# Linear attention and a gated MLP on one core: steps that wait for transfers issued turns later, weight decoding and VectorE steps pinned, transfers of a head pair merged

## The chip, the cores and the metric

One core of a Trainium2 chip runs the whole program. The metric is the device time of one execution in microseconds; the median of three runs stands for a kernel.

## The reference, cut to what matters

```python
def phi(x):                                   # 8 batches, 8 heads, 576 tokens, head_dim 64
    proj = einsum('bhsd,df->bhsf', x, w_phi)  # 128 features
    proj = proj - max(abs(proj), axis=-1)
    return concatenate([exp(proj), exp(-proj)], axis=-1)
kv  = einsum('bhsf,bhsd->bhfd', phi(k), v)
z   = sum(phi(k), axis=2)
num = einsum('bhsf,bhfd->bhsd', phi(q), kv)
den = einsum('bhsf,bhf->bhs', phi(q), z) + 1e-6
x   = (num / den) as [4608 tokens, 512]
out = ((x @ w_a) * (x @ w_b)) @ w_out         # d_ff = 1536
```

## The kernel before, in words

The program has two parts. In the first, the attention of 32 head pairs (batch b, pair pr) is written as generators whose steps are placed by hand at "turns": `plan(unit, turns)` puts the next step of a unit at a turn, a pair starts 5 turns after the one before (4 from the eighth pair on). In the code's names `pk`, `kd`, `ke` are the k side, `kvps` the sum of features by values, `pq`, `p32`, `qe` the q side and `pn` the numerator with the denominator as its last row. Into the same loop go three other streams: the weights' decoding (they come as 64-bit numbers; each 128x512 slab `raw` needs one ScalarE and at least four VectorE instructions), the first third of the MLP (pass 0) in nine blocks of 512 tokens (`moe_block`: 24 matmuls for each of four slices of `pa` and `pb`, then 48 for `po`, 144 in all), and `ahead`, the decoding of the weights of passes 1 and 2 (tiles `w_1_`, `w32_1_`, `ws_1_`, `keep_1_` and the same with 2), whose results go to DRAM (`kept`). `PACE` says how many steps of MLP work a turn gets, `AHEAD_TURN` and `AHEAD_PACE` the same for `ahead`. In the second part, passes 1 and 2 run with a Winograd scheme in 12 blocks of 768 tokens (`pab`, `po`).

A token's division by its denominator goes through DRAM: `xun` and `den` are stored from `xn`, `reciprocals` loads `den` as 128x9 (`r`), adds and inverts it on VectorE and stores `rec`; `x_chunk` loads `xun` as `x32` and `rec` spread over 64 partitions as `rb`, multiplies, and keeps `x32` in SBUF for the block while a copy goes to `xnorm` for the later passes. A block can start when all pairs of its batches have gone through this.

The turns set only the order in which instructions are traced. A scheduler then orders each engine's queue by its own timing model and may move an instruction ahead of others on its engine. At run time each engine works its queue in order; all transfers are issued from SyncE's queue, also in order. So an instruction that waits for a transfer holds up all that stand behind it.

Of the kernel before, what the change touches and what calls it, by code (L numbers as in the profile page):

```python
# [58 lines left out]
def tile_kernel(ctx, tc, qT, km, kr, vm, vr, w_phi, w_a, w_b, w_out, out):  # L59
# [107 lines left out]
    def k_load(b, pr, a1, a2, ps, consts, st):  # L167
# [5 lines left out]
        nc.sync.dma_start(k32, km[b, pr])  # L173
# [134 lines left out]
    def q_side(b, pr, j, a1, a2, ps, consts, st):  # L308
# [29 lines left out]
        engine("q_sub", b).tensor_tensor(p32, p32, mb, op=ALU.subtract)  # L338
# [10 lines left out]
        xn = a2.tile([P, S], F32, tag="xn", name=f"xn_{u}")  # L349
        for i in range(2):  # L350
# [5 lines left out]
            nc.scalar.copy(xn[: D + 1, tok], pn[: D + 1, :HALF])  # L356
        nc.sync.dma_start(xun[b][h * D : (h + 1) * D], xn[:D])
        nc.sync.dma_start(den[b][h : h + 1], xn[D : D + 1])
        yield

    def reciprocals(b, pr, a1):
# [496 lines left out]
```

## Time and profile before

| | us |
|---|---|
| median of three runs (1341.44 to 1348.44) | 1345.29 |
| the profiled execution: its time / span of its records | 1340.29 / 1338.5 |
| TensorE busy in the span | 1244.7 |
| VectorE busy | 863.4 |
| ScalarE busy | 655.0 |
| mean granted TensorE clock | 0.974 |

TensorE's busy time contains modelled ends, so that it can't be read as work at its peak; a stretch in which it is idle or at a lower clock is still read from it. The attention runs from 0 to about 676 us, pass 0 of the MLP ends at about 766 us, and the two Winograd passes fill the rest.

### The profile page before, as it was taken

Reading aid. Unit: us, or ns where it says so; the run is one execution under the profiler, and the core shown is the slowest. Engines: PE = TensorE matmul, PEld = TensorE weight load, DVE = VectorE, ACT = ScalarE, POOL = GpSimd, SP = SyncE. Lnnn points to the kernel's source line nnn. Section 1 sums busy time; section 2 is a strip of 40 time slices with the busy share of each in tenths; the row PEclk is TensorE's granted clock in tenths of the full one; section 3 lists DMA queues with packets and bytes.
Section 4 is the critical chain, followed back from the end, with each engine's and each line's share of the span. In section 5 each row is a group of like instructions: output and inputs, shape, how many; then the busy total and the mean of one; then the engine's idle time right before and its main releaser. Section 6 shows DMA issues by size and latency. Waiting matters only on the chain.

```text
span 1338.5 us, 18144 instructions
## 1 busy us (share of the span) xinstructions
PE 1244.7 (93%) x6575; PEld 1087.6 (81%) x6575; DVE 863.4 (65%) x1285; ACT 655.0 (49%) x1199; POOL 155.9 (12%) x70
## 2 busy tenths in 40 slices
PE   7899989889889899999949989999999999999997
PEld 5556657668668788788838789999999999999997
DVE  7987779899878766676525154665566555556453
ACT  5765566777776777777613132332233323223320
POOL 3221121122222222222100000000000000000000
PEclk9989999989889899999979999999999999999999
DMA  7656676766765535444263524413428531332221
GB/s 214 193 159 200 195 251 179 215 194 188 230 199 164 152 105 158 117 107 119 79 239 123 187 80 130 125 53 108 140 86 300 182 119 58 119 118 72 71 95 71
DMA packets 144074, 197.25 MB, mean 147 GB/s; under 512 B 60976, under 2 KB 87728, under 8 KB 143984
## 3 DMA queue, kind: packets, MB, share of 16 engines
q1 hardware_dynamic: 143984, 196.09, 47.7%
q8 instruction: 52, 0.85, 0.3%
q14 instruction: 38, 0.31, 0.1%
HBM read 129.68 MB, written 66.36 MB: 146 GB/s over the span
## 4 chain that ended last, share of the span: by engine, by line
PE 62%; DMA 18%; DVE 10%; ACT 4%; issue 4%; SPq 2%; POOL 0%; DVEq 0%; ACTq 0%
PE pab L661 26%; PE po L711 15%; DMA rb<-rec 4%; PE kvps L275 4%; PE po L594 4%; PE pb L579 4%; PE pa L579 3%; PE pn L355 3%; DMA rec<-r 3%; DMA xun<-xn 3%; DMA r<-den 2%; PE pk L223 1%; DMA raw_b<-in_w_b 1%; PE pq L333 1%; DMA raw_a<-in_w_a 1%
## 5 line engine op out<-in xcount | busy, mean ns | idle before, releaser
L337 POOL PARTITION_ALL_REDUCE mb<-p x64 | 155.3, 2427 | 493.4 <-ACT p L334 435.9
L711 PE MATMUL po<-hh,back_o 128*128 128x384 f32 x768 | 172.5, 340 | 6.7 <-ACT hh L153 6.5
L711 PEld LDWEIGHTS po<-hh,back_o 128*128 128x128 f32 x768 | 137.3, 188 | 9.4 <-ACT hh L153 8.1
L579 PE MATMUL pa<-xh,w_a 128*128 128x512 f32 x288 | 108.2, 417 | 25.5 <-ACT xh L153 25.4
L275 PE MATMUL kvps<-ke,vaug 128*65 128x256 f32 x512 | 126.8, 389 | 1.0 <-ACT ke L237 1.0
L579 PE MATMUL pb<-xh,w_b 128*128 128x512 f32 x288 | 104.2, 408 | 0.0
L275 PEld LDWEIGHTS kvps<-ke,vaug 128*65 128x65 f32 x512 | 71.9, 142 | 39.1 <-issue 4.1
L711 PE MATMUL po<-hl,back_o 128*128 128x384 f32 x384 | 99.0, 339 | 0.0
L594 PE MATMUL po<-hh,w_o 128*128 128x512 f32 x288 | 95.0, 401 | 0.6 <-ACT o L597 0.6
L579 PEld LDWEIGHTS pa<-xh,w_a 128*128 128x128 f32 x288 | 55.5, 193 | 39.4 <-ACT xh L153 27.5
L153 ACT CAST hh<-h 128x768 fp32r<-128x768 f32 (+1 forms) x84 | 61.7, 745 | 45.9 <-DVE h L584 32.6
L717 DVE TENSOR_TENSOR o<-po,o 128x768 f32<-128x768 f32 x48 | 45.3, 954 | 56.5 <-DMA o<-part 48.9
L160 DVE TENSOR_TENSOR hl<-h,hh 128x768 fp32r<-128x768 f32 (+1 forms) x84 | 70.5, 846 | 12.5 <-ACT hh L153 12.5
L153 ACT CAST xth<-xs 128x1536 fp32r<-128x1536 f32 x24 | 35.5, 1480 | 86.6 <-PE pab L661 54.8
L160 DVE TENSOR_TENSOR xtl<-xs,xth 128x1536 fp32r<-128x1536 f32 x24 | 42.2, 1758 | 51.6 <-ACT xth L153 51.6
L160 DVE TENSOR_TENSOR qel<-qe,qeh 128x1152 fp32r<-128x1152 f32 x46 | 64.2, 1396 | 15.1 <-ACT qeh L153 14.9
L711 PEld LDWEIGHTS po<-hl,back_o 128*128 128x128 f32 x384 | 69.9, 188 | 0.0
L667 ACT COPY top<-pab 128x768 f32<-128x768 f32 x24 | 19.3, 803 | 100.9 <-PE pab L661 97.6
L341 ACT ACTIVATE qe<-p 128x576 f32<-128x576 f32 x64 | 43.9, 686 | 43.5 <-DVE qel L160 36.8
L594 PEld LDWEIGHTS po<-hh,w_o 128*128 128x128 f32 x288 | 53.7, 188 | 12.6 <-ACT o L597 0.9
L579 PEld LDWEIGHTS pb<-xh,w_b 128*128 128x128 f32 x288 | 54.5, 191 | 11.5
L546 DVE TENSOR_TENSOR x<-x,rb 128x512 f32<-128x512 f32 x36 | 27.4, 761 | 52.9 <-DMA rb<-rec 45.9
(198 smaller groups left out, 3187.9 us busy)
## 6 DMA issues: line engine op xcount, KB each, us to landing
x<-xnorm SPq DMA_DIRECT2D x48, 384.0 KB
o<-part SPq DMA_DIRECT2D x48, 384.0 KB
q<-in_qT SPq DMA_DIRECT2D x92, 144.0 KB
xun<-xn SPq DMA_DIRECT2D x64, 144.0 KB
xnorm<-x SPq DMA_DIRECT2D x36, 256.0 KB
part<-o SPq DMA_DIRECT2D x36, 256.0 KB
part<-o SPq DMA_DIRECT2D x24, 384.0 KB
out_x<-o SPq DMA_DIRECT2D x24, 384.0 KB
```

Source lines behind the costliest of these rows:

```text
L153: eng.copy(dst, src)
L160: eng_lo.tensor_tensor(lo, src, hi, op=ALU.subtract)
L275: nc.tensor.matmul(st["kv_ps", b, pr][:width, j], v_[:, j, :width], e_[:, j], start=(left == NFULL and j == 0 and n_ == 0), stop=(left == ...
L337: nc.gpsimd.partition_all_reduce(mb, p32, P, bass_isa.ReduceOp.absmax)
L341: nc.scalar.activation(e[:, 0], p32, AF.Exp)
L355: nc.tensor.matmul(pn[: D + 1, :HALF], kv_[:, 2 * j + s, :], e_[:, s, tok], **at)
L546: nc.vector.tensor_tensor(x32, x32, rb, op=ALU.mult)
L579: nc.tensor.matmul(acc, w_, x_, start=(k == 0), stop=(k == 3 * NCC - 1))
L594: nc.tensor.matmul(acc, w_, h_, start=(k == 0), stop=(k == 3 * SLICES - 1))
L661: nc.tensor.matmul(acc[to][:, i], w_, x_, skip_group_check=True, **at)
L711: nc.tensor.matmul(acc[cc][:, t], w_, h[:, t], **at)
L717: nc.vector.tensor_tensor(o, acc[cc], o, op=ALU.add)
```

## The change

What it does:

1. `reciprocals` no longer does its work in one turn. Its six steps (load of `r`; add and reciprocal; store of `rec` with the load of `x32`; load of `rb`; multiplication; store of `xnorm`) stand 1, 3, 4, 5, 7 and 8 turns after the pair's last q step (`REC_TURNS`), in the first batch 0, 1, 1, 1, 2 and 2 turns after it.
2. The multiplication is done once for a pair and 576 tokens, and blocks load their `x32` from `xnorm`; the next block's loads are issued in the middle of the one before, if that block is ready by then. A block that was not loaded ahead has two steps more.
3. `behind(loads, ...)` puts these transfers, in SyncE's queue, behind the newest load of q or k, and `behind(marks, ...)` puts the two VectorE steps behind the newest subtraction of `mb` on VectorE.
4. `pinned()` does the same for all that the loop issues as MLP work, decoding and `ahead`: their VectorE instructions come behind the newest such subtraction. What is issued after the attention's loop is not pinned.
5. `ahead` starts at turn 84 instead of 50, with one step a turn instead of 0.6.
6. `xun` and `den` are stored once for a pair instead of once for a head; the host turns the rows of `w_a` and `w_b` to match the new order.
7. q's second copy and the zeros around v's rest come from the host, so that one transfer loads what two did.
8. Blocks start 2 turns behind the last step of a batch instead of 8.

```diff
-DECODE_TURN, X_LAG, BLOCK_LAG = 2, 2, 8
+REC_TURNS0, REC_TURNS, X_TURNS = (0, 1, 1, 1, 2, 2), (1, 3, 4, 5, 7, 8), (2, 3)
+DECODE_TURN, BLOCK_LAG = 2, 2
 PACE0, PACE, PACE0_UNTIL = 0.35, 0.5, 34
-AHEAD_TURN, AHEAD_PACE = 50, 0.6
+AHEAD_TURN, AHEAD_PACE = 84, 1.0
...
-        engine("q_sub", b).tensor_tensor(p32, p32, mb, op=ALU.subtract)
+        marks.append(nc.vector.tensor_tensor(p32, p32, mb, op=ALU.subtract))
...
-            nc.scalar.copy(xn[: D + 1, tok], pn[: D + 1, :HALF])
-        nc.sync.dma_start(xun[b][h * D : (h + 1) * D], xn[:D])
-        nc.sync.dma_start(den[b][h : h + 1], xn[D : D + 1])
-        yield
+            nc.scalar.copy(xn[: D + 1, j, tok], pn[: D + 1, :HALF])
+        if j == 1:
+            nc.sync.dma_start(den[b][h - 1 : h + 1].unsqueeze(0), xn[D : D + 1])
+            nc.sync.dma_start(xun[b][pr * P : (pr + 1) * P].rearrange("(d h) s -> d h s", h=2), xn[:D])
+        yield
...
+    def behind(what, issue):
+
+        with tc.issue_after(what[-1].ins):
+            issue()
...
-        nc.sync.dma_start(r, den[b][hs].rearrange("h (a n) -> (h a) n", n=n))
-        nc.vector.tensor_scalar_add(r, r, EPS)
+        behind(loads, lambda: nc.sync.dma_start(r, den[b][hs].rearrange("h (a n) -> (h a) n", n=n)))
+        yield
+        behind(marks, lambda: nc.vector.tensor_scalar_add(r, r, EPS))
         nc.vector.reciprocal(r, r)
-        nc.sync.dma_start(rec[b][hs].rearrange("h (a n) -> (h a) n", n=n), r)
+        yield
+        behind(loads, lambda: nc.sync.dma_start(rec[b][hs].rearrange("h (a n) -> (h a) n", n=n), r))
+        x32 = a1.tile([P, S], F32, tag="x32", name=f"x32_{b}_{pr}")
+        nc.sync.dma_start(x32, xun[b][pr * P : (pr + 1) * P])
+        yield
+        rb = a1.tile([P, S], F32, tag="rb", name=f"rb_{b}_{pr}")
+        behind(loads, lambda: nc.sync.dma_start(rb, rec[b][hs].unsqueeze(0).broadcast_to([D, 2, S])))
+        yield
+        behind(marks, lambda: nc.vector.tensor_tensor(x32, x32, rb, op=ALU.mult))
+        yield
+        t = 0
+        while t < S:
+            g, t0 = divmod(b * S + t, GROUP)
+            m = min(S - t, GROUP - t0)
+            behind(loads, lambda: nc.sync.dma_start(xnorm[g][pr * P : (pr + 1) * P, t0 : t0 + m], x32[:, t : t + m]))
+            t += m
...
+            plan(reciprocals(b, pr, pools[0]), [t0 + Q_STEP + Q_TURNS[-1] + t for t in (REC_TURNS if b else REC_TURNS0)])
...
+                plan(x_first, [t0 + Q_STEP + Q_TURNS[-1] + t for t in X_TURNS])
...
+                plan(b, [t0 + Q_STEP + Q_TURNS[-1] + REC_TURNS[-1]])
...
-            nc.sync.dma_start(x32[:, dst], xun[b][c * P : (c + 1) * P, src])
...
-                nc.sync.dma_start(rb[i * D : (i + 1) * D, dst], rec[b][h : h + 1, src].broadcast_to([D, n]))
...
-        nc.vector.tensor_tensor(x32, x32, rb, op=ALU.mult)
-        nc.sync.dma_start(columns(xnorm, j * T1, T1)[:, c], x32)
+    def x_load(j, c):
+        x32 = xpool.tile([P, T1], F32, tag="x32", bufs=3, name=f"x32_0_{j}_{c}")
+        nc.sync.dma_start(x32, columns(xnorm, j * T1, T1)[:, c])
         return x32
...
+    def x_make(j, c, x32):
+
+        hl = [xpool.tile([P, T1], F32R, tag=f"x{k}", bufs=NCC, name=f"x{k}_0_{j}_{c}") for k in "hl"]
+        split(*hl, x32, nc.scalar, nc.vector)
+        block_x.setdefault(j, []).append(hl)
...
-            first_x.append(x_)
+            loaded = x_load(0, c)
+            yield
+            x_make(0, c, loaded)
             yield
...
-        xs = first_x if j == 0 else list(load_x(j))
-        hs = []
-        yield
+        if j > 0 and j not in block_x:
+            for c in range(0, NCC, 2):
+                loaded = [x_load(j, c + i) for i in range(2)]
+                yield
+                for i in range(2):
+                    x_make(j, c + i, loaded[i])
+        hs, xs, loaded = [], block_x.pop(j), []
...
+            if f == 1 and j + 1 < blocks[0]:
+                loaded = [x_load(j + 1, c) for c in range(3)]
...
+            if loaded:
+                x_make(j + 1, cc, loaded.pop(0))
+                if cc + 3 < NCC:
+                    loaded.append(x_load(j + 1, cc + 3))
...
+    def pinned():
+
+        return tc.issue_after(marks[-1].ins) if marks else nullcontext()
...
-            run(work, int(due))
-            due -= int(due)
-            if turn >= AHEAD_TURN:
-                due_ahead += AHEAD_PACE
-                while due_ahead >= 1:
-                    next(ahead, None)
-                    due_ahead -= 1
+            with pinned():
+                if work:
+                    run(work, int(due))
+                    due -= int(due)
+                else:
+                    due = 0.0
+                if turn >= AHEAD_TURN:
+                    due_ahead += AHEAD_PACE
+                    while due_ahead >= 1:
+                        next(ahead, None)
+                        due_ahead -= 1
```

TensorE around the numerators of heads 2 and 3 of batch 2 (`pn_2_2`, `pn_2_3`; numbers at names' ends are the program's). Before:

```order
L355 MATMUL pn_2_2_0_1664<-qeh_2_2_1524,kvh_2_1_1576 65x288 x2
L355 MATMUL pn_2_2_1_1672<-qeh_2_2_1524,kvh_2_1_1576 65x288 x2
L333 MATMUL pq_2_5_0_1729<-qs_2_5_1725,wh_118 128x288
L333 MATMUL pq_2_5_0_1729<-qs_2_5_1725,wl_119 128x288
L579 MATMUL pb_0_1_0_2035<-xh_0_1_3_1926,w_0_0_b_249 128x512
L579 MATMUL pa_0_1_1_2135<-xl_0_1_3_1927,w_0_1_a_311 128x512
L579 MATMUL pa_0_1_1_2135<-xh_0_1_3_1926,w_0_1_a_311 128x512
L579 MATMUL pb_0_1_1_2148<-xh_0_1_0_1884,w_0_1_b_400 128x512
L579 MATMUL pb_0_1_1_2148<-xl_0_1_0_1885,w_0_1_b_400 128x512
```

With the change, TensorE's queue at the same numerator:

```order
L331 MATMUL pq_2_5_1_1709<-qs_2_5_1701,wh_118 128x288
L331 MATMUL pq_2_5_1_1709<-qs_2_5_1701,wl_119 128x288
L355 MATMUL pn_2_2_0_1658<-qel_2_2_1508,kvh_2_1_1578 65x288 x2
L355 MATMUL pn_2_2_0_1658<-qeh_2_2_1507,kvl_2_1_1580 65x288 x2
L355 MATMUL pn_2_2_1_1666<-qel_2_2_1508,kvh_2_1_1578 65x288 x2
L355 MATMUL pn_2_2_1_1666<-qeh_2_2_1507,kvl_2_1_1580 65x288 x2
L296 MATMUL pt_2_2_1737<-ident_126,kvT_2_2_1735 128x65 x4
L222 MATMUL pk_2_3_2_1713<-wzh_122,kh_2_3_1542 128x256
L222 MATMUL pk_2_3_2_1713<-wzl_123,kh_2_3_1542 128x256
L222 MATMUL pk_2_3_2_1713<-wzh_122,kl_2_3_1543 128x256
L222 MATMUL pk_2_3_2_1713<-wzh_122,kh_2_3_1542 128x256
```

Before, 52 instructions of MLP block 1 (`pa_0_1`, `pb_0_1`) stand between `pn_2_2` and the first of `pn_2_4`; with the change none does, since block 1's first matmuls come only at head 6 of the batch: block 0 is done by then, and block 1, which was not ready in time to be loaded ahead, has its two loading steps first.

TensorE at the last numerator of the attention, `pn_7_7`, and what stands next (`pa_0_6` is block 6's). Before:

```order
L355 MATMUL pn_7_7_1_6563<-qel_7_7_6533,kvh_7_3_6458 65x288 x2
L355 MATMUL pn_7_7_1_6563<-qeh_7_7_6532,kvl_7_3_6460 65x288 x2
L579 MATMUL pa_0_7_1_6979<-xh_0_7_0_6900,w_0_1_a_311 128x512
L579 MATMUL pa_0_7_1_6979<-xl_0_7_0_6901,w_0_1_a_311 128x512
L579 MATMUL pa_0_7_1_6979<-xh_0_7_0_6900,w_0_1_a_311 128x512
L579 MATMUL pa_0_7_1_6979<-xh_0_7_1_6914,w_0_1_a_311 128x512
L579 MATMUL pa_0_7_1_6979<-xl_0_7_1_6915,w_0_1_a_311 128x512
L579 MATMUL pa_0_7_1_6979<-xh_0_7_1_6914,w_0_1_a_311 128x512
```

With the change, TensorE's queue at the same numerator:

```order
L592 MATMUL pa_0_6_0_6561<-xh_0_6_3_6512,w_0_0_a_197 128x512
L592 MATMUL pa_0_6_0_6561<-xl_0_6_3_6513,w_0_0_a_197 128x512
L355 MATMUL pn_7_7_0_6396<-qel_7_7_6345,kvh_7_3_6251 65x288 x2
L355 MATMUL pn_7_7_0_6396<-qeh_7_7_6344,kvl_7_3_6253 65x288 x2
L355 MATMUL pn_7_7_1_6404<-qel_7_7_6345,kvh_7_3_6251 65x288 x2
L355 MATMUL pn_7_7_1_6404<-qeh_7_7_6344,kvl_7_3_6253 65x288 x2
L592 MATMUL pa_0_6_0_6561<-xh_0_6_3_6512,w_0_0_a_197 128x512
L592 MATMUL pb_0_6_0_6574<-xh_0_6_0_6414,w_0_0_b_270 128x512
L592 MATMUL pb_0_6_0_6574<-xl_0_6_0_6415,w_0_0_b_270 128x512
```

Before, blocks 0 to 6 are done by then and block 7 follows, whose x needs the last pairs of batch 7; with the change the last numerator stands among the first matmuls of block 6, so that 133 of block 6's 144 matmuls come before block 7's first.

VectorE, rows of the decoding for pass 2 (`w_2_`, `w32_2_`, `ws_2_`, `keep_2_`). Before, around the subtraction for head 0 of batch 4 (`p32_4_0`):

```order
L424 SCALAR_TENSOR_TENSOR w_2_1_b_0_8274<-raw_2_2_b_8272,w_2_1_b_0_8274 128x512
L160 TENSOR_TENSOR keep_2_1_w22_2_1_a_8242<-w32_2_1_a_8017,keep_2_1_w22_2_1_a_8242 128x256
L467 TENSOR_TENSOR w32_2_1_b_8271<-w_2_1_b_0_8274 128x512
L338 TENSOR_TENSOR p32_4_0_2879<-p32_4_0_2879,mb_4_0_2978 128x576
L227 TENSOR_REDUCE m_4_1_0_2989<-pk_4_1_0_2981 128x4
L160 TENSOR_TENSOR qel_3_6_2810<-qe_3_6_2806,qeh_3_6_2809 128x1152
L228 TENSOR_TENSOR kd_4_1_0_2988<-pk_4_1_0_2981,m_4_1_0_2989 128x512
L160 TENSOR_TENSOR keep_2_1_b_w1_2_1_b_8442<-w32_2_1_b_8271,keep_2_1_b_w1_2_1_b_8442 128x512
L419 TENSOR_SCALAR w_2_1_b_1_8340<-w_2_1_b_1_8340 128x512
L421 SCALAR_TENSOR_TENSOR w_2_1_b_1_8340<-raw_2_3_b_8338,w_2_1_b_1_8340 128x512
L422 TENSOR_SCALAR w_2_1_b_1_8340<-w_2_1_b_1_8340 128x512
```

With the change, at the same subtraction:

```order
L227 TENSOR_TENSOR kd_4_1_0_2815<-pk_4_1_0_2808,m_4_1_0_2816 128x512
L161 TENSOR_TENSOR qel_3_6_2683<-qe_3_6_2679,qeh_3_6_2682 128x1152
L336 TENSOR_TENSOR p32_4_0_2750<-p32_4_0_2750,mb_4_0_2805 128x576
L383 TENSOR_TENSOR x32_3_1_2785<-x32_3_1_2785,rb_3_1_2821 128x576
L373 TENSOR_SCALAR r_3_2_2823<-r_3_2_2823 128x9
L374 RECIPROCAL r_3_2_2823<-r_3_2_2823 128x9
L166 TENSOR_TENSOR qs_4_2_2936<-q32_4_2_2819,qs_4_2_2936 64x576
L226 TENSOR_REDUCE m_4_1_2_2905<-pk_4_1_2_2897 128x4
```

and behind the attention's last split (`qel_7_7`):

```order
L161 TENSOR_TENSOR qel_7_7_6345<-qe_7_7_6341,qeh_7_7_6344 128x1152
L161 TENSOR_TENSOR keep_2_0_a_w1_2_0_a_6507<-w32_2_0_a_6381,keep_2_0_a_w1_2_0_a_6507 128x512
L441 TENSOR_SCALAR w_2_0_a_1_6444<-w_2_0_a_1_6444 128x512
L383 TENSOR_TENSOR x32_7_2_6394<-x32_7_2_6394,rb_7_2_6438 128x576
L443 SCALAR_TENSOR_TENSOR w_2_0_a_1_6444<-raw_2_1_a_6442,w_2_0_a_1_6444 128x512
L444 TENSOR_SCALAR w_2_0_a_1_6444<-w_2_0_a_1_6444 128x512
L446 SCALAR_TENSOR_TENSOR w_2_0_a_1_6444<-raw_2_1_a_6442,w_2_0_a_1_6444 128x512
L489 TENSOR_TENSOR w32_2_0_a_6381<-w_2_0_a_1_6444 128x512
L494 TENSOR_TENSOR ws_2_0_a_6500<-w32_2_0_a_6381 128x256
```

Counted over the whole queue, up to the subtraction for `p32_2_1`, from there to `p32_4_7`, from there to `p32_7_7`, and behind it: of pass 0's 72 decoding instructions all 72 stay in the first part; of pass 1's 92 there were 55, 37, 0 and 0, and are 0, 10, 79 and 3; of pass 2's 92 all stood in the second part, and all stand behind the attention now. Pass 2's decoding is traced behind the attention in both kernels; its slabs come through the same single buffer `raw` as pass 1's, and behind them.

## Rows read from the trace of the kernel before

**Rows 1.** The page: busy time, share of the span and instructions of each engine.

```profile
PE 1244.7 (93%) x6575; PEld 1087.6 (81%) x6575; DVE 863.4 (65%) x1285; ACT 655.0 (49%) x1199; POOL 155.9 (12%) x70
```

**Rows 2.** Windows by stage: PE, PEld, DVE, ACT, POOL busy, PEclk, DMA share, GB/s.

```profile
0.00:204.00 204.00, 179.45 (x768) 122.55 (x769) 158.19 (x286) 128.03 (x271) 50.44 (x27) 0.97 0.67 201
204.00:452.00 248.00, 225.74 (x1187) 181.39 (x1186) 214.38 (x331) 177.64 (x349) 53.10 (x22) 0.96 0.65 195
452.00:676.00 224.00, 216.69 (x1187) 177.71 (x1186) 146.90 (x210) 157.53 (x311) 52.41 (x21) 0.98 0.42 116
676.00:698.00 22.00, 2.21 (x10) 1.40 (x9) 2.49 (x7) 1.02 (x3) 0.00 (x0) 0.65 0.70 250
698.00:775.00 77.00, 71.98 (x309) 58.94 (x309) 28.23 (x46) 23.07 (x39) 0.00 (x0) 0.97 0.54 174
775.00:1338.00 563.00, 548.63 (x3120) 545.61 (x3120) 313.25 (x410) 167.69 (x230) 0.00 (x0) 0.99 0.35 112
```

**Rows 3.** Waits, 0 to 204 us: who waited for whom, total us, times, longest.

```profile
DVE x L546 <- DMA rb<-rec: 8.6, 5, 2.2
...
DVE r L366 <- DMA r<-den: 4.1, 4, 2.6
```

**Rows 4.** Waits, 204 to 452 us.

```profile
PE pq L333 <- DVE qs L165: 12.6, 4, 5.3
DVE r L366 <- DMA r<-den: 10.3, 8, 3.4
...
DVE x L546 <- DMA rb<-rec: 6.4, 4, 2.2
```

**Rows 5.** Waits, 452 to 676 us.

```profile
DVE r L366 <- DMA r<-den: 31.8, 12, 4.7
...
DVE x L546 <- DMA rb<-rec: 17.2, 6, 4.1
...
PE pq L333 <- DVE qs L165: 4.5, 1, 4.5
```

**Rows 6.** Windows of short stretches inside the attention; columns as in rows 2.

```profile
321.00:345.00 24.00, 22.64 (x121) 18.43 (x120) 23.01 (x39) 18.39 (x37) 4.97 (x2) 1.00 0.67 207
452.00:471.00 19.00, 14.47 (x80) 11.75 (x79) 13.68 (x20) 13.49 (x27) 4.28 (x2) 0.82 0.54 142
471.00:530.00 59.00, 59.00 (x325) 48.70 (x324) 41.87 (x59) 44.25 (x88) 15.51 (x6) 1.00 0.45 129
```

**Rows 7.** VectorE groups, 204 to 452 us: busy us, mean ns, idle before.

```profile
L424 DVE SCALAR_TENSOR_TENSOR w_o<-raw_o,w_o 128x512 f32<-128x512 uint32 x8 | 5.5, 689 | 0.2
...
L160 DVE TENSOR_TENSOR keep_b_sl_b<-ws_b,keep_b_sh_b 128x1024 fp32r<-128x1024 f32 x2 | 3.2, 1578 | 0.0
...
L472 DVE TENSOR_TENSOR ws_b<-w_b 128x256 f32<-128x256 f32 x2 | 0.8, 410 | 0.0
```

**Rows 8.** Timeline of VectorE, 455 to 466 us: start, length, instruction, idle before.

```profile
457.68 0.17 DVE L366 TENSOR_SCALAR r<-r 128x9 f32<-128x9 f32 x1 [3.07 <-DMA r<-den]
```

**Rows 9.** The chain that ended last, 675 to 776 us: start us, us, what.

```profile
682.54 2.82 DMA rec<-r
...
688.77 7.43 DMA rb<-rec
...
751.55 2.80 PE pb L579 x12
```

**Rows 10.** The same chain, 160 to 176 us.

```profile
171.19 3.18 DMA xnorm<-x
```

**Rows 11.** The same chain, a transfer of raw weights.

```profile
255.92 5.12 DMA raw_a<-in_w_a
```

**Rows 12.** Waits of ScalarE for raw weights, whole run.

```profile
ACT w_b L418 <- DMA raw_b<-in_w_b: 19.1, 10, 4.3
...
ACT w_o L418 <- DMA raw_o<-in_w_out: 13.8, 9, 3.4
...
ACT w_a L418 <- DMA raw_a<-in_w_a: 8.3, 7, 2.6
```

More of the change, by code (lines that the diff above doesn't have):

```diff
@@ L2 @@
 from collections import deque
-from contextlib import ExitStack
+from contextlib import ExitStack, nullcontext
 import concourse.bass as bass
@@ L172, in k_load @@
         k32 = a1.tile([P, n], F32, tag="k32", bufs=2, name=f"k32_{u}")
-        nc.sync.dma_start(k32, km[b, pr])
+        loads.append(nc.sync.dma_start(k32, km[b, pr]))
         v32 = vaug[i % 3]
@@ L197, in rest_load @@
         v32 = rvz[g % 2]
-        for r in range(2):
-            rows = slice(r * REST, (r + 1) * REST)
-            nc.sync.dma_start(v32[rows, r, :, :D], vr[b, g, rows])
+        nc.sync.dma_start(v32[:, :, :, :D], vr[b, g])
         yield
@@ L321, in q_side @@
             q32 = a2.tile([P, S], F32, tag="q32", name=f"q32_{u}")
-            for r in range(2):
-                nc.sync.dma_start(q32[r * D : (r + 1) * D], qT[b, h])
+            loads.append(nc.sync.dma_start(q32, qD[b, h]))
             yield
@@ L754, in run @@
                 steps -= 1
-    away, weights, places, first_x, done_ahead = {}, {}, {}, [], set()
+    away, weights, places, block_x, done_ahead, marks, loads, blocks = {}, {}, {}, {}, set(), [], [], [0]
     places_ps, wide_pools, later_pool = [0], [], []
@@ L770, in tile_kernel @@
                 n = (ready + 1) * S // T1
-                tasks[turn + BLOCK_LAG] = [moe_block(j, ps_moe) for j in range(blocks, n)]
-                blocks = n
+                tasks[turn + BLOCK_LAG] = [moe_block(j, ps_moe) for j in range(blocks[0], n)]
+                blocks[0] = n
             for t in sorted(tasks):
@@ L841, with turned @@
     vm = np.ascontiguousarray(vp[:, :, :, :n].reshape(B, H // 2, 2, n // P, P, D).transpose(0, 1, 4, 3, 2, 5))
[L842 removed]
+    vr = np.zeros((B, H // 4, 2, S - n, 2, 2, D), v.dtype)
+    for r in range(2):
+        vr[:, :, r, :, r] = vp[:, r::2, :, n:].transpose(0, 1, 3, 2, 4)
+    vr = vr.reshape(B, H // 4, 2 * (S - n), 2, 2, D)
+    def turned(w):
+        return np.ascontiguousarray(w.reshape(H // 2, 2, D, -1).transpose(0, 2, 1, 3)).reshape(w.shape)
     arrays = {
[L844 to L845 removed]
+        "qP": qP, "qD": qD, "km": km, "kr": kr, "vm": vm, "vr": vr, "w_phi": np.ascontiguousarray(w_phi),
+        "w_a": turned(moe_w_a).view(np.int64), "w_b": turned(moe_w_b).view(np.int64), "w_out": moe_w_out.view(np.int64),
     }
```

42 lines of the change are left out of this document (11 added, 31 removed).

## The prediction

> **What bounds the kernel now.** I read the busy times first [rows 1]: TensorE is busy for 1244.7 of 1338.5 us, no other engine for more than 863. All matmuls are the same with the change, so the time can only fall by what TensorE loses. Then the windows by stage [rows 2]. A stage's loss I reckon as its length less the busy time, plus (1 - granted clock) times its length, since a matmul at half clock takes twice as long:
>
> - 0 to 204: 204 - 179.45 = 24.6, and 0.03 x 204 = 6.1: 30.7 us
> - 204 to 452: 22.3 + 0.04 x 248 = 32.2 us
> - 452 to 676: 7.3 + 0.02 x 224 = 11.8 us
> - 676 to 698: 19.8 us, almost all of it
> - 698 to 775: 5.0 + 2.3 = 7.3 us; 775 to 1338: 14.4 + 5.6 = 20.0 us
>
> That is 122 us. The two Winograd passes are at their limit and the change doesn't touch them, so the question is the first 95 us of the list.
>
> What ends the waits there? Third view: the waits by stage. VectorE waits for `r` and `rb` in all three: 12.7 us [rows 3], 16.7 us [rows 4] and 49.0 us [rows 5]. The reader should see that the stage with most of these waits has the smallest loss: from 452 to 676 VectorE is busy for 146.9 of 224 us [rows 2], so 49 us of waiting fit into its slack, and between 471 and 530 TensorE isn't idle at all [rows 6]. From 204 to 452 it is busy for 214.4 us; with 16.7 of waits that is 231 of 248. In the stretch from 321 to 345 it is busy for 23.0 of 24 [rows 6], and TensorE's longest waits are for `qs`, a VectorE result, 12.6 us [rows 4]. So VectorE's queue is the bound of this stage, and the waits for transfers matter there because they stand in a full queue.
>
> What fills that queue? By the counts in the section on the change 129 decoding instructions, of which 92 are for pass 2. Their durations lie between 410 and 1578 ns, most near 689 [rows 7]; I take 0.65 us each.
>
> **The change part by part.**
>
> *Middle, 204 to 452.* 129 decoding instructions become 10: 119 x 0.65 = 77 us leave VectorE, and most of the 16.7 us of waits, since `r` and `rb` now have about two turns each. Its occupied time falls from 231 to about 138 us, and it no longer bounds. Four head pairs, though, get next to no MLP work (the first place shown is one), and attention alone doesn't fill TensorE: the stretch from 452 to 471, which holds one such pair, loses 4.5 + 0.18 x 19 = 7.9 us [rows 6]. At best such a pair loses nothing, as 471 to 530 does; in the 7.9 there is a 4.5 us wait of TensorE for `qs` [rows 5], and VectorE had stood 3.07 us at `r` some instructions ahead of that `qs` [rows 8], which goes. So I take 2.7 for each, nearer to the low end: 11 us, and 3 us for the seven other pairs. 32 becomes 14: **-18 us** (bounds -29, all losses gone, and +3, four pairs at 7.9 and 3).
>
> *First stage, 0 to 204.* 127 decoding instructions become 72: 55 x 0.65 = 36 us less of VectorE's 158, and 12.7 us of waits. Its start, where nothing else is ready, stays. I take a third of the loss: **-10 us** (bounds 0 and -20).
>
> *Late stage, 452 to 676.* 79 decoding instructions of pass 1 come in: 79 x 0.65 = 51 us. The waits of 49.0 us go. VectorE is occupied for 146.9 + 51 = 198 us instead of 195.9. Nothing changes in sum: **0 us** (bounds: -11.8, and +17 if the stage loses the share that 204 to 452 loses now, 13%).
>
> *Tail, 676 to 698.* The last numerator is now followed by 133 matmuls of block 6. By the pace of 12 in 2.80 us [rows 9] they take 31 us. Behind them stands block 7, which waits for the last pair's chain: store of `den`, `r`, `rec`, `rb`, product, then, new, the store of `xnorm` and its load. The chain took some 22 us (676 to 698) in the kernel before, with `rec` at 2.82 and `rb` at 7.43 us [rows 9]; the store of `xnorm` took 3.18 us [rows 10], the load is taken as the same: 28 us, just under 31. But pass 2's decoding is here now: 92 x 0.65 = 60 us come on top of 28.2 us of VectorE from 698 to 775 [rows 2], in about 100 us of three blocks. That is 88% full, as the middle stage was (86%), so it will cost something: between 0 and 13% of 100 us. I take 8. 19.8 becomes 8: **-12 us** (bounds -20 and -7).
>
> The page "DMA: Bandwidth & Descriptors" of the Trainium skill, section "Anatomy of one DMA", gives a transfer a fixed cost of about 2 us however small it is, which speaks against two more links in the chain; by its figure alone the two would cost 4 us, an estimate, and 26 us would still fit under block 6.
>
> *At nothing.* Merged stores and loads (`xun`, `den`, q, v's rest) take issues from SyncE's queue; SyncE's own time isn't on the path while TensorE is busy, which is the cover, and if that were gone the merged transfer of a pair would start when its second head is done, one q step later than the first head's did. The loads of x for pass 0 (36 of 256 KB) are new traffic; the share of the DMA engines in the stages is 0.67 and below. At the block's start VectorE has a step less, since the product is done before.
>
> **The sum.** -18 - 10 + 0 - 12 = -40 us. The profiled execution took 1340.29 us, 1.8 more than its span, so 1300 us; the median of the runs is 1345.29, 0.4% above it, and 1300.3/1340.29 x 1345.29 = **1305 us**.
>
> **The rivals.**
>
> *The queues run clean (A).* With no wait for a transfer in VectorE's queue every stage runs like 471 to 530. First stage -20, middle -29, late -8, tail -20: -77, 1268 us. For it: the losses are chains of waits, and a stall is followed by a slow clock. Against: the sparse pairs.
>
> *Sparse pairs stall (B).* Attention alone is a chain from engine to engine, and each pair without MLP work loses 7.9 us as from 452 to 471. Four in the middle give +3 there; in the late stage two in place of one, +8; with -10 and -12 that is -11 us: 1334 us. For it: the granted clock of 0.82 in that stretch, while VectorE was busy for only 13.7 of 19 us [rows 6], so that it wasn't VectorE's load that held TensorE. Against: the same stretch held waits that the change removes. "TensorE: Matmul & The Clock Gate" of the Trainium skill, section "What's actually happening", says that an engine which was idle gets half its clock pulses until it has been busy again; by that rule each hole is paid for twice, and the clock of 0.82 behind the idle time there agrees.
>
> *Nothing comes of it (C).* As B, and the decoding in the tail costs block 6 to 8 what the hole of 19.8 cost: -11 + 12 = +1, 1346 us.
>
> *The decoding in the tail binds (D), slower.* There is one `raw` buffer, so a slab's load starts when VectorE is done with the one before, and the decoding stands between the splits that TensorE's `po` matmuls need. A load took 5.12 us [rows 11]. If VectorE stood still for all of it 12 times, that is 61 us: -28 + (61 + 8 - 19.8) = +21, 1367 us. It turns the sign when more than 40 of the 61 us come through, 3.3 us of each load. Against: in the whole run before ScalarE, which is first to touch a slab, waited 41.2 us for 36 slabs [rows 12], 1.1 us each; 12 of these are 14 us, about my 8.
>
> **How the numbers follow.** The forecast has a chance of 0.57, A 0.19, B 0.09, C 0.07, D 0.08. A change of this kernel under 0.5% (6.7 us) can't be told from none. The forecast's own span is 1285 to 1325, its bounds not all at one end; the range, 1268 to 1336, takes in A and B and leaves out C and D. Faster by over 0.5% (under 1338.6): forecast, A and nearly all of B, 0.84. Within 0.5%: C and a rest, 0.08. Slower: D, 0.08.
>
> **What would show it.** In the changed profile: VectorE's waits for `r` and `rb` under 15 us in sum; its busy time per us falls in the second batch to the fourth (under 75%) and rises from the fifth on; the last numerator comes earlier than 676 us by some 60 us (145 MLP matmuls, 34 us at the pace of 12 in 2.80 us, moved behind it, and the 28 us of the first two stages); no idle stretch of TensorE over 5 us behind it. Wrong would be the middle term if the pairs without MLP work show a granted clock under 0.9, and the tail term if `pa` or `po` of blocks 6 to 8 wait for splits by more than 15 us, with VectorE waiting for slabs.

## The result, and the profile after

The changed kernel takes 1293.78 us in the median of four runs (1289.77 to 1296.88), the kernel before 1346.87 beside it: a ratio of 0.961, interval 0.957 to 0.965. 1305 was predicted, in a range of 1268 to 1336. The profiled execution took 1292.23 us; its span is 48 us shorter than the 1338.5 of before.

The page of the changed kernel: the span, then busy time and share of each engine.

```profile
span 1290.4 us, 17768 instructions
PE 1234.2 (96%) x6575; PEld 1086.4 (84%) x6575; DVE 862.1 (67%) x1281; ACT 658.3 (51%) x1199; POOL 152.8 (12%) x70
```

The windows of the changed kernel, cut where the same heads end as in [rows 2]: the first three stages, the tail in two pieces, the Winograd passes.

```profile
0.00:188.00 188.00, 165.81 (x733) 115.57 (x734) 122.04 (x211) 116.20 (x248) 49.26 (x27) 0.97 0.59 171
188.00:381.00 193.00, 186.39 (x1058) 152.89 (x1057) 152.59 (x223) 154.19 (x306) 50.97 (x22) 0.99 0.60 174
381.00:612.00 231.00, 223.12 (x1203) 181.72 (x1202) 194.76 (x300) 172.76 (x338) 52.60 (x21) 0.98 0.67 197
612.00:700.00 88.00, 85.68 (x371) 68.75 (x370) 64.48 (x117) 38.63 (x65) 0.00 (x0) 1.00 0.81 284
700.00:742.00 42.00, 33.69 (x139) 28.61 (x138) 15.75 (x26) 10.88 (x18) 0.00 (x0) 0.84 0.65 220
742.00:1290.00 548.00, 539.48 (x3079) 538.84 (x3077) 312.54 (x408) 165.69 (x226) 0.00 (x0) 0.99 0.36 114
```

By the prediction's formula (length less TensorE's busy time, plus (1 - clock) times length) TensorE's losses are now, with those of before in brackets: first stage 27.8 (30.7), middle 8.5 (32.2), late stage 12.5 (11.8), tail 2.3 + 15.0 = 17.3 (27.1), passes 14.0 (20.0). That is 80 after 122. The clock is read to 0.01, which is 2 us in a stage of 200 and 5.5 us in the passes. The middle gave most of it. VectorE's share there fell from 86% to 79%, and rose from 66% to 84% in the late stage, as the decoding moved.

The losses explain 42 of the 48 us; the lengths close the account. ScalarE has copied the last numerator of the attention at 611.6 us, after 676.1 before. 145 MLP matmuls now come behind it that came ahead of it, 34 us at the pace of [rows 9], an estimate; so the first three stages gained 31 us. From there to the matmul at which TensorE's wait for `top` ends (the passage to the Winograd passes) it is 120.6 us, after 99.3; without the 34 us that is a gain of 12.5. The 3120 matmuls from that one to the end take 558.2 us, after 563.2: a gain of 5.0. Together that is the 48 us. TensorE's waits for `hh` in the passes, the kernel before and then the changed one:

```profile
PE po L711 <- ACT hh L153: 6.5, 5, 2.1
```

```profile
PE po L730 <- ACT hh L154: 2.1, 1, 2.1
```

VectorE's waits for `r` and `rb` in the changed kernel, one stage after the other (total us, times, longest).

```profile
DVE r L373 <- DMA r<-den: 4.9, 4, 3.2
DVE x L383 <- DMA rb<-rec: 4.2, 3, 1.9
...
DVE r L373 <- DMA r<-den: 6.2, 7, 1.7
...
DVE r L373 <- DMA r<-den: 5.1, 3, 2.5
DVE x L383 <- DMA rb<-rec: 1.7, 1, 1.7
```

They are 22 us in the whole run, after 78 in the three stages [rows 3 to 5] (94 with the tail); the late stage holds 6.8 after 49.0. TensorE's own waits in the changed kernel: for block 0's x in the first stage; for `qs` in the middle and the late stage; in the tail.

```profile
PE pa L592 <- ACT xh L154: 7.2, 2, 6.2
...
PE pq L331 <- DVE qs L166: 1.0, 2, 0.5
...
PE pq L331 <- DVE qs L166: 5.3, 3, 2.3
...
PE po L613 <- ACT o L616: 3.9, 1, 3.9
PE pab L680 <- ACT top L686: 3.7, 1, 3.7
```

The 12.6 us for `qs` in the middle [rows 4] have become 1.0. One wait has grown: TensorE's longest wait for block 0's `xh` in the first stage was 2.0 us before and is 6.2 now, as that x goes through the store of `xnorm` and a load.

### The profile page after: what moved, and what is told of

Its sections match the earlier page's. It is cut to its first block, busy times and chain, and to the rows that moved or that the text cites. A ratio compares the mean times of both kernels' runs of the same rounds, so it can differ in the third digit from the quotient of the medians.

```text
span 1290.4 us, 17768 instructions
## 1 busy us (share of the span) xinstructions
PE 1234.2 (96%) x6575; PEld 1086.4 (84%) x6575; DVE 862.1 (67%) x1281; ACT 658.3 (51%) x1199; POOL 152.8 (12%) x70
## 4 chain that ended last, share of the span: by engine, by line
PE 74%; DMA 10%; DVE 8%; issue 3%; ACT 3%; POOL 1%; SPq 0%; POOLq 0%; DVEq 0%; ACTq 0%
PE pab L680 27%; PE po L730 16%; PE kvps L274 8%; PE pn L355 5%; PE pa L592 5%; PE pb L592 5%; PE po L613 4%; PE pk L222 2%; PE pq L331 2%; DMA x<-xnorm 1%; DMA raw_o<-in_w_out 1%; DMA rec<-r 1%; DMA rb<-rec 1%; DMA xnorm<-x 1%; DVE qs L166 1%
## 5 line engine op out<-in xcount | busy, mean ns | idle before, releaser
L335 POOL PARTITION_ALL_REDUCE mb<-p x64 | 152.2, 2379 | 429.0 <-ACT p L332 370.5
L592 PE MATMUL pa<-xh,w_a 128*128 128x512 f32 x288 | 101.4, 407 | 7.2 <-ACT xh L154 7.2
L613 PE MATMUL po<-hh,w_o 128*128 128x512 f32 x288 | 99.0, 410 | 5.1 <-ACT o L616 3.9
L592 PE MATMUL pb<-xh,w_b 128*128 128x512 f32 x288 | 98.4, 398 | 1.5 <-ACT h L596 1.5
L730 PE MATMUL po<-hl,back_o 128*128 128x384 f32 x384 | 99.3, 339 | 0.0
L161 DVE TENSOR_TENSOR qel<-qe,qeh 128x1152 fp32r<-128x1152 f32 x46 | 64.6, 1405 | 16.6 <-ACT qeh L154 16.3
L686 ACT COPY top<-pab 128x768 f32<-128x768 f32 x24 | 19.3, 803 | 105.3 <-PE pab L680 102.9
L166 DVE TENSOR_TENSOR qs<-q,qs 64x576 fp32r<-64x576 f32 x46 | 52.0, 1131 | 28.1 <-ACT qs L154 27.2
L690 ACT COPY top<-pab 128x768 f32<-128x768 f32 x24 | 19.2, 802 | 97.0 <-PE pab L680 97.0
L226 DVE TENSOR_REDUCE m<-pk 128x4 f32<-128x512 f32 x64 | 44.0, 688 | 32.7 <-PE pk L222 32.1
L592 PEld LDWEIGHTS pb<-xh,w_b 128*128 128x128 f32 x288 | 54.1, 188 | 13.9 <-ACT h L596 1.7
```

The lines of the kernel that those rows point to most:

```text
L161: eng_lo.tensor_tensor(lo, src, hi, op=ALU.subtract)
L166: eng_lo.tensor_tensor(hi_lo[D:], src[D:], hi_lo[D:], op=ALU.subtract)
L226: nc.vector.tensor_reduce(out=m[:, : 2 * n], in_=p, op=ALU.max, axis=AX.X, apply_absolute_value=True)
L335: nc.gpsimd.partition_all_reduce(mb, p32, P, bass_isa.ReduceOp.absmax)
L592: nc.tensor.matmul(acc, w_, x_, start=(k == 0), stop=(k == 3 * NCC - 1))
L613: nc.tensor.matmul(acc, w_, h_, start=(k == 0), stop=(k == 3 * SLICES - 1))
```

## The experiments

Two theories. *Queue*: what counts is which instructions stand in VectorE's and ScalarE's queues ahead of those that TensorE waits for; the decoding's way out of the middle is the gain. *Waits*: the gain is that no step waits for a transfer in VectorE's queue, which the spreading does. Ratios are to the kernel before on the same chip; where microseconds are worked out from them, 1340 stands for it. The changed kernel was run once more with the last set. Each edit also lets the scheduler write another order on the other engines, so a run shows the edit with the order that came of it.

| run | median us | ratio [interval] | losses: first, middle, late, tail, passes |
|---|---|---|---|
| before | 1340 to 1347 | 1 | 30.7, 32.2, 11.8, 34.7, 20.0 |
| change | 1293.78 | 0.961 [0.957, 0.965] | 27.8, 8.5, 12.5, 17.1, 14.0 |
| change_again | 1287.77 | 0.961 [0.959, 0.963] | 24.8, 8.6, 11.0, 13.9, 14.3 |
| decode_back | 1321.66 | 0.986 [0.982, 0.990] | 20.2, 30.6, 4.0, 29.7, 20.3 |
| decode_alone | 1300.85 | 0.970 [0.967, 0.973] | 19.3, 18.0, 22.0, 9.0, 14.2 |
| spread_back | 1322.04 | 0.986 [0.981, 0.990] | 32.3, 29.9, 28.9, 9.6, 14.0 |
| unmerged | 1302.61 | 0.972 [0.969, 0.975] | 25.8, 19.4, 10.2, 10.0, 19.7 |
| q_two | 1294.85 | 0.966 [0.963, 0.970] | 31.4, 8.7, 10.6, 14.0, 14.4 |
| x0_direct | 1301.44 | 0.970 [0.967, 0.973] | 26.0, 19.2, 10.8, 11.7, 9.2 |
| held_early | 1299.71 | 0.969 [0.966, 0.973] | 28.8, 18.8, 10.6, 9.7, 8.8 |
| p2_late | 1297.05 | 0.967 [0.965, 0.970] | 28.6, 8.5, 12.5, 8.4, 20.2 |
| p2_slow | 1309.31 | 0.977 [0.975, 0.979] | 30.9, 10.5, 11.0, 10.4, 30.6 |
| qs_behind | 1305.28 | 0.974 [0.971, 0.976] | 29.1, 21.2, 14.2, 16.4, 13.6 |
| blocks_free | 1318.64 | 0.984 [0.981, 0.986] | 16.8, 10.5, 22.7, 43.1, 20.5 |

The losses are by the formula, each kernel cut at its own heads, the tail in one window (so 34.7 for before, where two windows give 27.1). The two profiles of the changed kernel differ by 3 us in the first stage and the tail. p2_late, p2_slow, held_early and qs_behind have its first stage instruction by instruction, and over these six profiles that stage loses 24.8 to 30.9 us: a difference under 6 us there shows nothing. The losses don't add up to the medians, since both terms of the formula count idle time at half clock.

**decode_back.**

```diff
-AHEAD_TURN, AHEAD_PACE = 84, 1.0
+AHEAD_TURN, AHEAD_PACE = 50, 0.6
...
-        return tc.issue_after(marks[-1].ins) if marks else nullcontext()
+        return nullcontext()
```

> The changed kernel with the decoding of the later passes back at turn 50 at a pace of 0.6 and nothing of it held behind a named instruction: 129 decoding instructions stand on VectorE between the last numerators of batches 1 and 4 again, and none in the tail. Spread steps and merged transfers stay. First theory (the gain is VectorE's queue emptied of decoding): about 1322 us, 28 slower than the 1294 of the change; from batch 2 to 4 VectorE is busy for over 85% of the time and TensorE's loss there is 25 us or more again, against 8.5 with the change. Rival (the gain is that no step waits for a transfer in VectorE's queue): about 1302, since the steps stay spread; TensorE's loss in that stage stays under 15 us.

33 us of 52 go (0.9857 - 0.9611 of 1340): *queue* got its number. The middle and the tail, cut from this run's windows:

```profile
187.00:424.00 237.00, 215.91 (x1150) 174.43 (x1148) 205.30 (x321) 174.08 (x343) 52.11 (x23) 0.96 0.69 210
...
649.00:741.00 92.00, 74.62 (x319) 60.22 (x317) 26.90 (x44) 22.45 (x38) 0.00 (x0) 0.91 0.51 168
```

VectorE is at 87% in the middle and TensorE loses 30.6 us, though the steps are still spread and VectorE waits only 6.2 us for `r` there. The hole behind the last numerator is back as well (17.4 us for `xh`), with 16 matmuls of block 6 behind that numerator in place of 133. The edit frees the blocks' steps too; blocks_free, below, frees them alone, and there the hole comes back while the middle loses 10.5. So the hole is theirs, and the middle's loss is the decoding's, with ScalarE's order that came with it (qs_behind). One more thing shows in the order of instructions alone: with the named instructions left out and the numbers 84 and 1.0 kept, each engine's order is line for line that of this kernel. The table of turns does nothing by itself here; the named instruction moves the decoding.

**decode_alone.** The kernel before, with

```diff
-AHEAD_TURN, AHEAD_PACE = 50, 0.6
+AHEAD_TURN, AHEAD_PACE = 84, 1.0
...
-            run(work, int(due))
...
+            with pinned():
+                run(work, int(due))
...
```

> The kernel before, with this alone: the decoding starts at turn 84 at a pace of 1.0, and decoding and blocks' VectorE steps are held behind the last subtraction. The reciprocals, the products in the blocks and the transfers are as before. First theory: about 1318 us, with 10 decoding instructions left in batches 2 to 4, TensorE's loss there 12 us or less, though VectorE still waits for r and rb there. Rival: 1335 to 1346 us, the loss stays 25 or more. As x for block 7 must be made from the last rec inside the block, the hole behind the last numerator should be shorter than 19.8 us by either theory, since matmuls of earlier blocks now stand there.

Three quarters of the gain (0.970), more than *queue* expected. The edit does two things, it moves the decoding and holds the blocks' steps. The middle loses 18.0, not 12, the first stage 19.3. But the late stage, with decoding and waits both in it (VectorE waits 45 us for `r` and `rb` in the whole run, 16 of them there), loses 22.0 in place of 11.8.

**spread_back.**

```diff
-REC_TURNS0, REC_TURNS, X_TURNS = (0, 1, 1, 1, 2, 2), (1, 3, 4, 5, 7, 8), (2, 3)
+REC_TURNS0, REC_TURNS, X_TURNS = (0,) * 6, (0,) * 6, (2, 3)
...
-        with tc.issue_after(what[-1].ins):
-            issue()
+        issue()
...
```

> The changed kernel with the six steps of the reciprocals in one turn and none of them held behind a named instruction; a batch's blocks still start at the same turn. First theory: 1294 to 1302 us; VectorE waits for r and rb come back (40 us or more in sum, most in the late stage), but lie in its slack. Rival: 1320 us or more, with TensorE losing 25 us or more from batch 2 to 4.

*Waits* got its number: 33 us lost, in the middle (29.9) and in the late stage (28.9). Two rows of VectorE's waits in the middle, and the window of that stage:

```profile
DVE x L382 <- DMA rb<-rec: 16.1, 9, 5.9
DVE r L372 <- DMA r<-den: 11.7, 8, 3.4
```

```profile
191.00:405.00 214.00, 196.98 (x1066) 158.97 (x1065) 150.53 (x224) 153.79 (x307) 53.38 (x22) 0.94 0.56 158
```

VectorE is busy for 70% there, 83% with these waits, so that waits can cost as much in a queue that isn't full. One of the two casts named below, that of (4,2), stands behind here as well. The whole run has 73 us of waits for `r` and `rb`. The change puts the product with `rb` into the attention's queue, where the kernel before had it in the blocks. So the spreading isn't a gain over the kernel before, it is what the new place of the product needs: decode_alone, which has neither, is 21 us faster than this one.

**unmerged, q_two.**

```diff
-            loads.append(nc.sync.dma_start(q32, qD[b, h]))
+            for r in range(2):
+                loads.append(nc.sync.dma_start(q32[r * D : (r + 1) * D], qD[b, h, :D]))
...
-        if j == 1:
-            nc.sync.dma_start(den[b][h - 1 : h + 1].unsqueeze(0), xn[D : D + 1])
+        nc.sync.dma_start(den[b][h : h + 1], xn[D : D + 1, j])
```

(the store of `xun` and the rest of v alike; q_two has the first part alone).

> The changed kernel with the transfers of before in place of the merged ones: q in two transfers of 64 rows, the rest of v in two, and each head's numerator and denominator stored when that head is done. Both theories: within 6 us of 1294, since SyncE's queue is not on TensorE's path. A third theory (the merging shortens the chain that TensorE waits for) gives 1305 us or more.

> The changed kernel with q alone loaded in two transfers of 64 rows again. If it was q that cost the 10 us in the middle when all transfers were undone (TensorE's waits for qs, 8 us there): 1300 us or more. If it was the stores of xun and den, or only another order that came with them: 1291 to 1297 us.

Unmerged is 14 us slower than the change, which looked like the third theory. But its middle loses 19.4, and TensorE's longest waits there are again for `qs`, 10.3 us, not for a transfer. The orders of the two kernels differ in where ScalarE's cast to `qs` of heads (2,6) and (4,2) stands: ahead of a cast to `qeh` in the change and in q_two, behind it in unmerged, and in x0_direct, which has merged transfers and the same loss. That asked for a run of its own:

**qs_behind.**

```diff
+LATE_QS = ((2, 6), (4, 2))
...
-            stack(qs, q32, engine("q_hi", b), nc.vector)
+            with tc.issue_after(qeh[b * H + h - 3].ins) if (b, h) in LATE_QS else nullcontext():
+                stack(qs, q32, engine("q_hi", b), nc.vector)
...
```

> The changed kernel with two instructions queued later: ScalarE's cast to qs of heads (2,6) and (4,2) behind the cast to qeh of the head three before, which is where the kernels with undone transfers and with block 0's x straight from SBUF have them; in the change they stand ahead of it. Theory (the 10 us that those two kernels lost from batch 2 to 4 are this order, no transfer): TensorE waits 2 to 4 us for qs at each and at the heads behind, that stage's loss goes from 8.5 to 16 us or more, 8 us slower than the change in the same set. Rival (the order is only a sign of something else, late stores or loads): within 3 us of the change.

ScalarE's timeline at head (2,6), the changed kernel first, then this one:

```profile
193.51 0.69 ACT L154 CAST qs<-q 128x576 fp32r<-128x576 f32 x1
194.08 0.70 ACT L356 COPY xn<-pn 65x288 f32<-65x288 f32 x2
194.66 1.17 ACT L154 CAST qeh<-qe 128x1152 fp32r<-128x1152 f32 x1
```

```profile
193.53 0.93 ACT L362 COPY xn<-pn 65x288 f32<-65x288 f32 x2
194.36 1.15 ACT L347 CAST qeh<-qe 128x1152 fp32r<-128x1152 f32 x1
195.42 0.67 ACT L155 CAST qs<-q 128x576 fp32r<-128x576 f32 x1
```

The cast begins 1.9 us later, and TensorE waits in this stage (188 to 394) for `qs`, 3.4 us at each of the two places (198.5 and 309.0) and 3.7 at 215.9, behind the first:

```profile
PE pq L333 <- DVE qs L167: 12.6, 6, 3.7
```

Its granted clock over the stage falls from 0.99 to 0.96, as the two rows show (change_again, qs_behind).

```profile
185.00:378.00 193.00, 186.37 (x1059) 152.83 (x1058) 152.22 (x223) 154.23 (x306) 51.37 (x22) 0.99 0.60 173
```

```profile
188.00:394.00 206.00, 193.02 (x1062) 157.55 (x1061) 153.59 (x222) 153.80 (x305) 50.40 (x22) 0.96 0.58 164
```

The middle loses 21.2 after 8.6, and the run 17 us. The order is enough; a late transfer isn't needed. What is shown is the two casts together with the order that the scheduler then wrote: 219 of TensorE's 1416 instructions up to the end of batch 4 stand elsewhere too. It costs only where no block's matmul fills in: blocks_free has the two casts behind as well, and its middle, which has block matmuls there, loses 10.5. What q alone is worth stays open: q_two's interval touches that of the change, and it ran on another chip.

**x0_direct.** Block 0's x is split from the product in SBUF.

```diff
+        if b == 0:
+            x_make(0, pr, x32[:, :T1])
+            yield
...
-                plan(x_first, [t0 + Q_STEP + Q_TURNS[-1] + t for t in X_TURNS])
```

> The changed kernel, in which block 0's x is split right from the normalised pair in SBUF: the store of xnorm and its load no longer stand in that chain (the store stays, for the later passes). Theory (the first stage gained only little because the change put two more transfers ahead of block 0): TensorE's wait of 6.2 us for xh at 107.8 us and the half clock around it go, 1286 us. Rival (the first stage is bound by attention's own chain, and the wait only covers other ones): 1291 to 1297 us.

The wait of 6.2 us for `xh` is gone, and the first stage still loses 26.0: TensorE waits 5.4 us at once for `kvh` now. The rival is right for that stage. The run is slower than it expected, and its middle, with the two casts behind, loses 19.2: the other order came with the edit.

**held_early.** `AHEAD_TURN, AHEAD_PACE = 50, 0.6`, all else as changed.

> The changed kernel with the decoding at turn 50 and a pace of 0.6 as before, but held behind the last subtraction as in the change: 40 decoding instructions in batches 2 to 4 in place of 14, placed evenly, and fewer in batches 5 to 7. Theory (the load on VectorE counts): the middle loses about 5 us more and the late stage 3 less, 1294 to 1299 us. Rival (it isn't the load but that hoisted decoding stands ahead of urgent steps): no loss at all in the middle, and 1288 us or less, since the late stage is relieved.

The middle of this run:

```profile
188.00:393.00 205.00, 190.33 (x1064) 154.31 (x1063) 168.93 (x250) 158.26 (x314) 51.55 (x22) 0.98 0.64 184
```

It loses 18.8, so the load counts even if evenly placed, twice as much as I had reckoned: 26 more decoding instructions, 16.3 us more of VectorE (168.9 after 152.6), cost 10 us. The two casts stand ahead here as in the change, so it isn't their order. Whether VectorE's share does it, or ScalarE's (4 us more of work and 3.8 us of waits for slabs), isn't separated. The late stage loses 10.6, no less than in the second profile of the change (11.0).

**blocks_free.**

```diff
-            with pinned():
-                if work:
-                    run(work, int(due))
...
+            if work:
+                run(work, int(due))
...
+            with pinned():
                 if turn >= AHEAD_TURN:
```

> The changed kernel with the MLP blocks' VectorE steps (and pass 0's decoding) no longer held behind the last subtraction; the later passes' decoding still is. Behind the last numerator stand 30 matmuls of block 6 in place of 133, before blocks 7 and 8. Theory (the tail's gain comes from the blocks' matmuls that were held back): a hole of 14 to 18 us behind block 6 comes back, 1303 to 1310 us. Rival (the tail is short because the chain behind the last numerator is shorter): a hole under 6 us, 1290 to 1298 us.

31 us slower, and the hole is larger than expected: 23.7 us for `xh` up to 672 us. The chain that ended last, cut to the load at its end; then SyncE's queue ahead of that load:

```profile
662.69 8.61 DMA x<-xnorm
671.32 0.62 ACT xh L154
```

```profile
656.83 0.32 SPq L389 DMA_DIRECT2D xnorm<-x  x1
658.66 0.38 SPq L457 DMA_DIRECT2D raw_a<-in_w_a  x1
659.21 0.38 SPq L527 DMA_DIRECT2D back_a_w<-kept_a_w  x1
...
662.16 0.49 SPq L527 DMA_DIRECT2D back_b_sl<-kept_b_sl  x1
662.69 1.88 SPq L555 DMA_DIRECT2D x<-xnorm  x3
```

The last numerator is done at 635.4, so its chain to `xh` takes 36 us. In the changed kernel the same chain takes 34 us: the last numerator is done at 611.6, the last pair's product is stored from 629.84 on, x is loaded from 636.27 on, and ScalarE casts it at 645.57.

```profile
629.84 0.32 SPq L389 DMA_DIRECT2D xnorm<-x  x1
...
636.27 1.58 SPq L555 DMA_DIRECT2D x<-xnorm  x3
```

```profile
645.57 0.62 ACT L154 CAST xh<-x 128x512 fp32r<-128x512 f32 x1 [4.00 <-DMA x<-xnorm]
```

TensorE doesn't notice it there, with 133 matmuls of block 6 in front. The chain is as long in both, and the held matmuls are the difference: the theory holds for the tail. Both chains are longer than the 28 us of the prediction; in both, six loads of decoded weights (`back`, 512 KB each) are issued right ahead of the last load of x, here with a slab before them. Not all of the 31 us is the hole, for the late stage loses 22.7, 10 to 12 more than with the change, with TensorE's waits for `qs` in three stretches without a block's matmul:

```profile
PE pq L331 <- DVE qs L166: 12.8, 3, 5.2
```

The first stage, on the other hand, loses 16.8, 8 to 11 less than with the change. Holding the blocks' steps doesn't cost that by itself, as decode_alone holds them too and loses 19.3 there; it costs it beside the product's new place.

**p2_late, p2_slow.** Pass 2's decoding behind the Winograd passes' own steps (p2_slow with `SECOND_PACE = 0.55` besides):

```diff
-        nc.vector.tensor_tensor(top[:, 0], acc[1], top[:, 0], op=ALU.add)
+        late_marks.append(nc.vector.tensor_tensor(top[:, 0], acc[1], top[:, 0], op=ALU.add))
...
+        with tc.issue_after(late_marks[-1].ins):
+            while due >= 1:
```

> The changed kernel with the decoding of pass 2 held behind VectorE's instructions of the first Winograd pass: of its 92 VectorE instructions 76 go from the tail into that pass, with their loads. Theory (the decoding costs the tail the 8 us of the prediction): TensorE's waits of 3.9 us for o and 3.7 us for top go, 1286 us. Rival (these waits belong to the passage from blocks to passes, which lost 4.8 us in the kernel before too): 1292 to 1298 us, and the first Winograd pass, in which VectorE is busy for 57%, loses up to 3.

> As the run with pass 2's decoding held in the first Winograd pass, but at a pace of 0.55 in place of 1.0: 16, 17, 17, 14 and 12 of the 76 VectorE instructions in its first five blocks in place of 21, 35 and 20 in three. Theory (the passes lost there because decoding crowded the first two blocks): the waits for hh of 6 us in sum near 803 and 854 us go, and the tail keeps its 5 us: 4 us or more faster than the change in the same set. Rival (any decoding instruction ahead of a split costs the pass the same wherever it stands): as slow as the run before, 2 to 4 us slower than the change.

The tail of p2_late loses 8.4 in place of 17.1 (13.9 in the second profile), so the decoding did cost it 6 to 9. The passes lose 20.2 and 30.6 in place of 14.0; from the wait for `top` to the end they take 567.8 and 578.6 us in place of 558.2. Both runs are slower than the change, by 8 and 21 us. In p2_slow TensorE waits there as follows; below it, at its first such wait, ScalarE (which stood 4.1 us at a slab's load).

```profile
PE po L730 <- ACT hh L154: 15.6, 9, 4.1
```

```profile
803.85 0.67 ACT L440 ACTIVATE w_a<-raw_a 128x512 f32<-128x512 f32 x1 [4.14 <-DMA raw_a<-in_w_a]
804.83 1.47 ACT L154 CAST xth<-xs 128x1536 fp32r<-128x1536 f32 x1 [0.31 <-PE pab L680]
...
808.52 0.83 ACT L154 CAST hh<-h 128x768 fp32r<-128x768 f32 x1 [1.84 <-DVE h L702]
```

My theory of crowding falls: thinner decoding over five blocks costs more than the same over three. The tail is the cheapest place of the three that were tried.

## Why the prediction was right, point by point

*The bound.* Right for the kernel before: the full queue of the middle, not the waits, was the loss. VectorE waits 6.2 us for `r` and `rb` in the middle of decode_back, 16.7 in the kernel before, and the middle loses the same (30.6 and 32.2). It isn't the only way to lose it: in spread_back's middle VectorE has room, and the waits that stand ahead of the attention's steps cost TensorE 29.9.

*Middle, -18; measured -24.* The step that was mis-sized is what is left. I took 14 us, 2.7 for each sparse pair and 3 for the rest; 8.5 are left. Three fifths of the way is the decoding (decode_alone 18.0). The rest is, at least in part, two casts that the scheduler put ahead: they stand behind before and in decode_alone, and putting them back takes 8.6 to 21.2 (qs_behind). I didn't see them in the order though they were there to be read. What the spreading adds to that in the middle isn't separated. 62 us left VectorE, not 77, as the window before held 113 decoding instructions and the new one holds 18, where I had counted 129 and 10 by other cuts; the price of 0.65 us was right (75.5 us in 113). Its share is 79%, over the 75 that I had set as a sign. The bound of -29, called all losses gone, left 3 us of the 32.

*First stage, -10; measured 0 to -6.* Too much, and with the spread of 6 us no gain is shown at all. decode_alone gains 11 and blocks_free 14, so the relief is real, but the change takes it back: with the product in the attention's queue and the blocks' steps held, not with either alone. How isn't separated; the new store and load ahead of block 0 are not enough to explain it (x0_direct, 26.0).

*Late stage, 0; measured +1 or -1.* Right, and by the sum as put: waits out, decoding in. With the decoding in and the waits not out it loses 22.0 (decode_alone) or 28.9 (spread_back), 10 and 17 more than before; the second is the upper bound of +17.

*Tail, -12; measured -12.5 by its length, -16 in the second profile (-10 by the windows).* The cover is what does it (blocks_free). The chain is 34 us, not 28: the two new links, store and load of x, take 15.7 us from the store's issue (629.84) to the cast (645.57), where I took 6.4. 133 matmuls at the pace of [rows 9] are 31 us, and block 7 starts on the first three pairs' x. The price of the decoding, 8, was 6 to 9.

*Passes, 0; measured -5 by their length (-6 by the windows).* "The change doesn't touch them" was wrong. TensorE's waits for `hh` are 6.5 us in five places before, in unmerged, in decode_back and in blocks_free, and 2.1 in one place with the change: the scheduler wrote another order of `pab` and `po`. What tips it was not found.

*The sum.* -40 was forecast and the span fell by 48, the median by 53. That it came so near is in part luck: the first stage gave 4 to 10 us less than its term, and the middle (6 more) and the passes (5, put at nothing) made up for it by orders of the scheduler that I had not foreseen.

*The signs.* The last numerator comes 64.5 us earlier (60 said). The waits for `r` and `rb` are 22 us, not under 15. No idle stretch behind it is over 5 us (3.9), and `po` waits 5.1 us there, not 15. The two stretches of the middle without MLP matmuls (184.9 to 223.1 and 289.6 to 311.4 us) have a granted clock of 0.96 and 1.00, over the 0.9 that was set; the one at the start of the late stage (377.9 to 402.7) has 0.86, and 0.93 in the second profile.

*The rivals.* B falls for the change, and C with it; but what B describes is real: where `qs` comes late, the pairs without MLP matmuls stall, in the middle of qs_behind and of spread_back and in the late stage of blocks_free. D's mechanism exists (ScalarE at the slab's load in p2_slow), but in the tail it costs what I took, not 61 us. A falls: the late stage kept its loss, and so did the first.

## What to carry to other kernels

Take filler work out of the queue of the engine that the bound engine waits for, and check the written order, not the table that asks for it: here the turns moved nothing without a named instruction to queue behind. Read where each operand of a starving stage stands in its engine's queue: two casts held 1.9 us, with the order that came of it, cost 17 us. A step that waits for transfers cost little in the late stage before (49.0 us of waits, 11.8 lost) and much in spread_back, where it stands ahead of the attention's own steps. Slack in the waiting engine didn't make it free, so spread it when its result, or the work queued behind it, is what the bound engine needs.

## What the runs showed of the hardware

Of the loads of 256 KB issued from 662.69 on behind seven of 512 KB, the one that TensorE needed landed 8.61 us later (blocks_free), against 3.18 for the store in [rows 10]. The Trainium skill's page "DMA: Bandwidth & Descriptors", section "Anatomy of one DMA — SWDGE (gpsimd) path", has a fixed 2 us and a part that grows with the bytes, for transfers that GpSimd issues; taken over to one that SyncE issues, with nothing else under way, 256 KB would take 2.6 us, an estimate. The row differs, and the row decides.

The subtraction that makes `qs` (64x576), for which TensorE waits in the middle, takes 0.75 to 0.76 us in the 18 of its 46 places in the changed kernel that don't lie wholly inside one of GpSimd's all-reduces (`mb`), and 0.76 to 1.74, 1.37 in the mean, in the 28 that do. The trace of the kernel before shows the same, 1.49 in the mean inside. So what GpSimd does beside it is part of what VectorE's queue holds; no run here tests what that costs.
